# Moving two of the four attention visits in the second layer: from steps 13.5 and 21.5 to 17.5 and 24

## The chip, the cores and the metric

The kernel runs on one core of one Trainium2 chip. The metric is the device time of one execution in microseconds. Three runs of the kernel before gave a median of 938.7 us (937.01 to 938.94). The engines are named as in the profile: PE multiplies matrices (PEld loads its weights), ACT, DVE and POOL work element by element, SP issues all DMAs of the stretch that matters here.

## The reference

What is computed is causal attention with a window of 128 keys and a distance bias, for 8 sequences of 576 tokens and 8 heads of 64, and behind it a two-layer network with a mish-like gate, for all 4608 tokens (512 to 2048 to 512 wide). Cut to what matters:

```python
scores = scale * q @ k.T                       # per head, scale = 1/sqrt(64)
scores = where((rel >= 0) & (rel < 128), scores + bias, -1e9)
attn   = softmax(scores)
x      = (attn @ v)  -> [4608, 512]
h      = x @ w_in                              # 512 -> 2048
g      = h * tanh(softplus(h))
out    = g @ w_out                             # 2048 -> 512
```

## The kernel before

**Tiling.** The network takes 512 tokens at a time: one chunk `c` per sequence, 0 to 7, and a ninth chunk of the 64 tokens that are left over from each sequence. Every fp32 operand is split into a high and a low part, and three products of the parts are added up, so each layer of a chunk is 192 matmuls of 128x512. The first layer (`first`, tile `h`) makes 8 pairs of feature blocks `j`. `mish` turns `h` into `g` (ACT). `parts` splits `g` into `gg`: a high part by ACT, a low part by POOL.

**The second layer and its steps.** `second(c, half, j, t)` does six matmuls `po <- so, gg`. The 512 tokens are taken as two halves of 256, and each half as two tiles `t` of 128; a half runs through all 8 `j` with both tiles before the next half begins. So there are 32 steps of six matmuls, numbered 2m + t, where m counts 8 j's of half 0 and then 8 of half 1. Steps 0 to 15 are half 0, steps 16 to 31 half 1. The place between steps 15 and 16 is called the seam here. Each tile `t` has one bank of PSUM (`po0`, `po1`, one buffer each), so half 1 can begin to add into `po0` only when the finished sums of half 0 have been copied out of it. That copy is `store(c, half, t)`: at j = 7 it copies `po` into `ob` (for half 0 both copies are on ACT) and issues the DMA of `ob` to the output. `parts` of m stands in the program at step 2m - 4.1; `gg` has three buffers.

**The attention beside it.** While chunk c is multiplied, the attention of sequence c + 1 is done beside it, for c = 1 to 6, six layers in all. It has four pairs of heads, p = 0 to 3. For a pair: `scores` (matmuls into PSUM tile `s`), `block_bias` (DVE), `block_exp` (ACT), `divide`, `scale` (POOL), `squares_out` (a DVE transpose by 32x32 blocks, then four DMAs of `pz` to a DRAM tile `d`, two for each of two groups), `squares_in` (two DMAs of `d` back into the one buffer `pt`, in another arrangement), `values` (matmuls `o`, `w` <- `pt`, `v`), `keep` and `split_x` (copies out of PSUM). Pairs 0 and 1 are begun beside the first layer, pairs 2 and 3 beside the second. The second layer is interrupted at four places, the visits, where PE does attention matmuls: the first has the values of pair 0 and the scores of pair 2, the second the values of pair 1 and the scores of pair 3, the third the values of pair 2, the fourth the values of pair 3.

**What sets the order.** Each piece of attention has a place x in pairs, and `when(x)` maps it onto steps of the second layer, straight between the four entries of `VISITS`. The pieces and the steps are then sorted by step and written out. PE and SP keep that order (`InOrder` with `fixed`); ACT, DVE and POOL are put in order by a scheduler that goes by estimated times.

```python
steps = [(-0.001, both_scores)]
steps += [(0.01 + 0.05 * g, f) for g in range(2) for x in zip(biases[g], exps[g]) for f in x]
steps += [(0.12 + 0.09 * g, lambda g=g: weights(g)) for g in range(2)]
steps += [(0.3 + 0.15 * g, lambda g=g: squares_out(g)) for g in range(2)]
steps += [(1.005, squares_in)]
return [(p - 2 + d, f) for d, f in steps] + ends
```

These are the lines for pairs 2 and 3. `ends` are `values` at p, `keep` at p + 0.008 and `split_x` at p + 0.009. Apart from the visits, `load_v` of pair 3 stands at the fixed step 17.5. Its buffer (tag `x3`) was used by `ob` of half 0, so the load waits on SP until both output DMAs of half 0 have landed.

Of the kernel before, what the change touches and what calls it, by code (L numbers as in the profile page):

```python
# [80 lines left out]
def attention_mish_mlp(  # L81
# [225 lines left out]
    def load_pair(b, p):  # L307
        t = at.tile([P, 2 * S], F32, tag="qk", name=f"qk{b}_{p}")
        load(t, qk_[b, p][:, : 2 * S])
        qkv[(b, p)] = parts_of(t)  # L310

    def load_v(b, p):

        if b > 1:
            t = xp.tile([P, 7, P], F32, tag=f"x{p}", name=f"v{b}_{p}", bufs=1)
            load(t, v[b, p, :, :7])
            qkv[("v", b, p)] = t
            return
        if (b, p) == (0, NP - 1):
            t = begin[:, :1024].rearrange("p (a k n) -> p a k n", a=2, k=4)  # L320
        else:
            t = xp.tile([P, 2, 4, P], F32, tag=f"x{p}", name=f"v{b}_{p}", bufs=1)
        load(t.rearrange("p a k n -> p (a k) n"), v[b, p])
        qkv[("v", b, p)] = ((t[:, 0], t[:, 1]), t[:64, 1, 3])
# [654 lines left out]

    def attention(b):  # L980

        VISITS = (5.5, 13.5, 21.5, 29.9)

        def when(x):
            k = min(max(int(x // 1), 0), 2)
            return VISITS[k] + (VISITS[k + 1] - VISITS[k]) * (x - k)

        def next_pair(p):
            nxt = (b, p + 2) if p + 2 < NP else (b + 1, p + 2 - NP)
            if nxt[0] < B:  # L990
                load_pair(*nxt)

        ahead, steps = {}, []
        for p in range(NP):
            if p > 1:
                steps += pair_steps(b, p) + [(p - 1.993, lambda p=p: next_pair(p))]
                continue
            before, beside, behind, squares_in, ends = pair_steps(b, p)

            ahead[4 + 2 * p] = (before + [lambda p=p: next_pair(p)], beside, behind)  # L1000
            if p:
                steps.append((0.005, squares_in))
            else:
                ahead[5] = ([], [], [squares_in])
            steps += ends
        steps = [(when(x), f) for x, f in steps]

        steps += [(d, lambda p=p: load_v(b, p)) for p, d in enumerate((-0.5, -0.4, 6.5, 17.5))]
        return ahead, sorted(steps, key=lambda s: s[0])
# [175 lines left out]

    for c in range(1, B + 1):
        ahead, steps_beside = attention(c + 1) if c + 1 < B else ({}, [])
        for j in range(NJ):
            before, beside, behind = ahead.get(j, ([], [], []))
# [119 lines left out]
```

## Time and profile before

| | |
|---|---|
| median of three runs | 938.7 us |
| the profiled execution, its own time | 938.49 us |
| its span in the trace | 936.8 us |
| PE busy | 921.8 us, 98% of the span |
| ACT, POOL, DVE busy | 436.1, 337.9, 287.1 us |
| granted PE clock | full in all 40 slices |

About 1.7 us of the profiled time lie outside the span. To read it: PE is the engine that is never free for long, and matmuls of one kind follow each other in a pipe, so the trace shows each with some 390 ns while they start about 227 ns apart. What a place costs is read from the starts of matmuls, not from their shown lengths. Where PE sat idle, the row names in square brackets how long and what ended it.

### The profile page before, as it was taken

To read this page: it belongs to the slowest core of one execution; us is meant where nothing else is said; L and a number is where in the kernel's file an instruction comes from. 1 tells how busy PE (TensorE), PEld (TensorE's weight loads), DVE (VectorE), ACT (ScalarE), POOL (GpSimd) and SP (SyncE) were. 2 spreads that over 40 slices of the span, in tenths; PEclk is the share of its full clock that TensorE was granted. 3 is DMA by queue.
4 is the path that set the end of the run, shared out by engine and by line. 5 is a ranking of instruction groups with operands and counts; after the bars stand their busy time and mean duration, and the time that the engine had idled before them with its cause. 6 is when DMAs were issued, how large, how long until landed. Compare 5 with 4: busy or idle time off the path is not lost.

```text
span 936.8 us, 17458 instructions
## 1 busy us (share of the span) xinstructions
PE 921.8 (98%) x6842; PEld 755.6 (81%) x6842; DVE 287.1 (31%) x1095; ACT 436.1 (47%) x1075; POOL 337.9 (36%) x300
## 2 busy tenths in 40 slices
PE   8999999999999999999999999999999999999997
PEld 7788788887888788887888788878888788888886
DVE  5998760433023511332043302251042300100000
ACT  6999653744255623653265425461364422322221
POOL 4587741245123521254123512262124410331042
PEclk9999999999999999999999999999999999999999
DMA  9973210457124740546044721564055510000001
GB/s 345 392 281 116 96 54 25 127 148 216 46 65 140 205 128 15 176 137 184 25 126 120 226 65 43 162 170 140 23 157 144 160 47 1 23 23 23 0 23 24
DMA packets 79379, 108.23 MB, mean 116 GB/s; under 512 B 9280, under 2 KB 59456, under 8 KB 79296
## 3 DMA queue, kind: packets, MB, share of 16 engines
q1 hardware_dynamic: 79296, 107.11, 37.4%
q8 instruction: 54, 0.88, 0.4%
q14 instruction: 29, 0.24, 0.1%
HBM read 75.37 MB, written 31.72 MB: 114 GB/s over the span
## 4 chain that ended last, share of the span: by engine, by line
PE 89%; ACT 5%; DMA 3%; DVE 1%; issue 1%; SPq 0%; POOL 0%; ACTq 0%; DVEq 0%
PE h L69 41%; PE po L69 39%; ACT pz L69 3%; PE s L69 2%; PE o L69 2%; DMA wi<-in_moe_w_in_dram 1%; PE po0s L69 1%; PE w L69 1%; PE os L69 1%; DMA nl<-in_rell_dram 1%; DMA first<-in_qkb_dram 1%; ACT to L69 0%; ACT so L69 0%; ACT ob L69 0%; DVE to L69 0%
## 5 line engine op out<-in xcount | busy, mean ns | idle before, releaser
L69 PE MATMUL po<-so,gg 128*128 128x512 f32 x1728 | 405.5, 392 | 6.3 <-ACT ob L69 6.3
L69 PE MATMUL h<-x,si 128*128 128x512 f32 x1728 | 398.1, 390 | 0.0
L69 PEld LDWEIGHTS po<-so,gg 128*128 128x128 f32 x1728 | 321.2, 188 | 77.3 <-ACT ob L69 8.9
L69 PEld LDWEIGHTS h<-x,si 128*128 128x128 f32 x1728 | 323.0, 188 | 70.3 <-issue 3.3
L69 POOL TENSOR_TENSOR gg<-g,gg 128x512 fp32r<-128x512 f32 x144 | 185.1, 1288 | 404.5 <-ACT gg L69 404.5
L69 ACT ACTIVATE gg<-g 128x512 fp32r<-128x512 f32 x144 | 90.6, 630 | 183.9 <-PE po L69 181.8
L69 ACT ACTIVATE g<-h 128x1024 f32<-128x1024 f32 x72 | 74.0, 1028 | 193.5 <-PE h L69 193.4
L69 POOL TENSOR_TENSOR pz<-pz,sm 128x768 f32<-128x768 f32 (+3 forms) x72 | 99.0, 1384 | 128.2 <-DVE sm L69 118.5
L69 ACT ACTIVATE pz<-pz,mx 128x192 f32<-128x192 f32 (+1 forms) x280 | 120.2, 430 | 10.5 <-DVE mx L69 10.1
L69 DVE CUSTOM_DVE_ANT_0 pz<-s,nb 128x192 f32<-128x192 f32 (+1 forms) x160 | 46.7, 327 | 101.7 <-PE s L69 99.9
L69 DVE STREAM_TRANSPOSE pz<-pz 128x768 f32<-128x768 f32 (+1 forms) x48 | 51.2, 1067 | 18.0 <-POOL pz L69 18.0
L69 DVE CUSTOM_DVE_ANT_0 pz<-os,nb 128x192 f32<-128x192 f32 x24 | 8.5, 355 | 150.3 <-PE ws L69 150.3
L69 ACT ACT_TABLE_LOAD x39 | 50.0, 1283 | 5.7 <-DVE mx L69 5.3
L69 ACT ACTIVATION_READ_ACCUMULATOR pz<-pz,mx 128x1 f32 x280 | 52.3, 187 | 0.0
L69 DVE COPY ob<-po 128x512 f32<-128x512 f32 x10 | 6.9, 692 | 137.3 <-PE po L69 137.3
L69 PE MATMUL w<-pt,v 64*64 64x64 f32 (+1 forms) x864 | 41.1, 239 | 0.0
L69 DVE COPY xo<-w 128x64 f32<-128x64 f32 x24 | 5.4, 225 | 115.1 <-PE w L69 114.8
L69 PE MATMUL o<-pt,v 64*64 64x64 f32 (+1 forms) x768 | 40.4, 248 | 0.0
L69 PEld LDWEIGHTS o<-pt,v 64*64 64x64 f32 x768 | 36.8, 133 | 4.3 <-issue 4.2
L69 PEld LDWEIGHTS w<-pt,v 64*64 64x64 f32 x864 | 37.7, 133 | 0.0
L69 ACT ACTIVATE x<-o 128x256 fp32r<-128x256 f32 (+1 forms) x32 | 12.9, 403 | 43.5 <-PE w L69 42.9
L69 ACT ACTIVATE ob<-po 128x512 f32<-128x512 f32 x26 | 14.9, 599 | 34.1 <-PE po L69 34.1
(183 smaller groups left out, 581.1 us busy)
## 6 DMA issues: line engine op xcount, KB each, us to landing
qk<-in_qk_dram SPq DMA_DIRECT2D x28, 576.0 KB, 5.6
d<-pz SPq DMA_DIRECT2D x48, 240.0 KB, 3.4
pt<-d SPq DMA_DIRECT2D x24, 480.0 KB, 5.9
v<-in_v_dram SPq DMA_DIRECT2D x24, 448.0 KB, 4.4
d<-pz SPq DMA_DIRECT2D x48, 192.0 KB, 2.9
pt<-d SPq DMA_DIRECT2D x24, 384.0 KB, 4.3
wi<-in_moe_w_in_dram SPq DMA_DIRECT2D x16, 512.0 KB, 10.7
wo<-in_moe_w_out_dram SPq DMA_DIRECT2D x16, 512.0 KB, 10.2
```

The costliest lines, as they stand in the source:

```text
L69: ins = method(*args, **kwargs)
```

## The change

One line: the second visit moves from between steps 13 and 14 to between steps 17 and 18, and the third from between steps 21 and 22 to behind step 24. The first (5.5) and the fourth (29.9) stay.

```diff
     def attention(b):
 
-        VISITS = (5.5, 13.5, 21.5, 29.9)
+        VISITS = (5.5, 17.5, 24.0, 29.9)
 
         def when(x):
             k = min(max(int(x // 1), 0), 2)
             return VISITS[k] + (VISITS[k + 1] - VISITS[k]) * (x - k)
```

Everything that `when` places between the visits moves with them. Counted in steps of the second layer, the stretches between visits were 8, 8 and 8, and become 12, 7 and 5.

On ACT, at the end of half 0, the second visit of the layer beside sequence 2 stood thus before. `pz2_3` are the exponentials of pair 3, `gg1_1_1` the high part for half 1, j = 1, and `ob1_0` the output copies of half 0:

```order
L69 ACTIVATE gg1_1_0_2404<-g1_0_1775 128x512
L69 ACTIVATE gg1_1_1_2502<-g1_0_1775 128x512
L69 ACTIVATE pz2_3_0_2430,sm2_3_0_2429<-pz2_3_0_2430,mx2_3_0_2428 128x6x32 x4
L69 ACTIVATE pz2_3_1_2444,sm2_3_1_2443<-pz2_3_1_2444,mx2_3_1_2442 128x6x32
L69 ACTIVATE sm2_3_0_2429<-sm2_3_0_2429 128x4
L69 ACTIVATE pz2_3_1_2444,sm2_3_1_2443<-pz2_3_1_2444,mx2_3_1_2442 128x6x32 x2
L69 ACTIVATE pz2_3_1_2444,sm2_3_1_2443<-pz2_3_1_2444,mx2_3_1_2442 128x4x32 x2
L69 ACTIVATE sm2_3_1_2443<-sm2_3_1_2443 128x5
L69 ACTIVATE x2_1_2489<-o2_1_2445 128x256
L69 ACTIVATE x2_1_2489<-w2_1_2446 128x2x128
L69 ACTIVATE ob1_0_2524<-po1_0_0_2202 128x512
L69 ACTIVATE ob1_0_2524<-po1_0_1_2209 128x512
```

The same stretch of ACT after the change:

```order
L69 ACTIVATE gg1_1_0_2404<-g1_0_1775 128x512
L69 ACTIVATE gg1_1_1_2419<-g1_0_1775 128x512
L69 ACTIVATE ob1_0_2428<-po1_0_0_2202 128x512
L69 ACTIVATE ob1_0_2428<-po1_0_1_2209 128x512
L69 ACTIVATE gg1_1_2_2439<-g1_1_1893 128x512
L69 ACTIVATE gg1_1_3_2554<-g1_1_1893 128x512
L69 ACTIVATE pz2_3_0_2467,sm2_3_0_2466<-pz2_3_0_2467,mx2_3_0_2465 128x6x32 x4
L69 ACTIVATE pz2_3_1_2481,sm2_3_1_2480<-pz2_3_1_2481,mx2_3_1_2479 128x6x32
```

The two output copies now stand ahead of the exponentials and of the copies of `x2_1`, not behind them; two casts of `gg` come between.

On SP, where a DMA that waits holds up all that stand behind it, the same layer had this order before. `d02_3` and `d12_3` are the two groups of pair 3 in DRAM, `pt2_3` their load back, `v2_3` the values of pair 3, `qk3_1` the queries and keys of a pair of the next sequence:

```order
L69 DMA d02_2_2370<-pz2_2_0_2257 128x3x128 x2
L69 DMA d12_2_2386<-pz2_2_1_2271 128x3x160 x2
L69 DMA pt2_2_2481<-d02_2_2370 64x4x384
L69 DMA pt2_2_2481<-d12_2_2386 64x4x480
L69 DMA qk3_1_2484<-in_qk_dram 128x1152
L69 DMA xs_95<-xo2_1_2486 128x64
L69 DMA out_0_dram<-ob1_0_2524 128x512 x2
L69 DMA d02_3_2546<-pz2_3_0_2430 128x3x128 x2
L69 DMA d12_3_2564<-pz2_3_1_2444 128x3x160 x2
L69 DMA v2_3_2567<-in_v_dram 128x896
L69 DMA pt2_3_2635<-d02_3_2546 64x4x384
L69 DMA pt2_3_2635<-d12_3_2564 64x4x480
```

And after:

```order
L69 DMA d02_2_2382<-pz2_2_0_2257 128x3x128 x2
L69 DMA d12_2_2395<-pz2_2_1_2271 128x3x160 x2
L69 DMA out_0_dram<-ob1_0_2428 128x512 x2
L69 DMA v2_3_2518<-in_v_dram 128x896
L69 DMA pt2_2_2520<-d02_2_2382 64x4x384
L69 DMA pt2_2_2520<-d12_2_2395 64x4x480
L69 DMA qk3_1_2523<-in_qk_dram 128x1152
L69 DMA xs_95<-xo2_1_2525 128x64
L69 DMA d02_3_2577<-pz2_3_0_2467 128x3x128 x2
L69 DMA d12_3_2590<-pz2_3_1_2481 128x3x160 x2
L69 DMA pt2_3_2659<-d02_3_2577 64x4x384
L69 DMA pt2_3_2659<-d12_3_2590 64x4x480
```

The output DMAs and the load of `v2_3` move from between the transfers of pair 3 to ahead of the load of `pt2_2`.

## Rows read from the trace of the kernel before

**Rows 1.** The page: the span, and one group of instructions.
```profile
span 936.8 us, 17458 instructions
...
L69 PE MATMUL po<-so,gg 128*128 128x512 f32 x1728 | 405.5, 392 | 6.3 <-ACT ob L69 6.3
```
**Rows 2.** Who waited for whom, whole span: us in total, times, longest us.
```profile
PE po L69 <- ACT ob L69: 6.3, 6, 1.2
```
**Rows 3.** Timeline of PE beside sequence 3: start us, us, what, [idle before].
```profile
305.07 11.18 PE L69 MATMUL po<-so,gg 128*128 128x512 f32 x48
316.18 1.57 PE L69 MATMUL s<-qk 64*64 64x192 f32 x33
...
319.21 3.02 PE L69 MATMUL po<-so,gg 128*128 128x512 f32 x12
323.25 8.46 PE L69 MATMUL po<-so,gg 128*128 128x512 f32 x36 [1.03 <-ACT ob L69]
331.64 0.32 PE L69 MATMUL o<-pt,v 64*64 64x128 f32 x1
...
333.16 11.20 PE L69 MATMUL po<-so,gg 128*128 128x512 f32 x48
```
**Rows 4.** The chain of work that ended last: a second layer without attention.
```profile
801.50 43.52 PE po L69 x192
```
**Rows 5.** Timeline of ACT, same layer as rows 3.
```profile
316.34 0.63 ACT L69 ACTIVATE gg<-g 128x512 fp32r<-128x512 f32 x1 [2.09 <-PE po L69]
317.53 0.46 ACT L69 ACTIVATE pz<-pz,mx 128x192 f32<-128x192 f32 x1 [0.56 <-DVE mx L69]
...
322.61 1.08 ACT L69 ACTIVATE ob<-po 128x512 f32<-128x512 f32 x2
```
**Rows 6.** Timeline of POOL, same layer.
```profile
324.31 1.29 POOL L69 TENSOR_TENSOR gg<-g,gg 128x512 fp32r<-128x512 f32 x1
```
**Rows 7.** Timeline of SP's DMA issues: start us, us to issue, what.
```profile
312.87 0.53 SPq L69 DMA_DIRECT2D d<-pz  x1
...
319.35 1.71 SPq L69 DMA_DIRECT2D pt<-d  x2
...
326.87 0.55 SPq L69 DMA_DIRECT2D d<-pz  x1
...
333.30 0.58 SPq L69 DMA_DIRECT2D pt<-d  x1
334.32 1.32 SPq L69 DMA_DIRECT2D pt<-d  x1
```
**Rows 8.** DMAs issued 326.85 to 329: packets and rate; KB, us to landing.
```profile
DMA packets 898, 0.80 MB, mean 370 GB/s; under 512 B 128, under 2 KB 662, under 8 KB 898
...
d<-pz SPq DMA_DIRECT2D x1, 240.0 KB, 5.4
```
**Rows 9.** Larger load of `pt`, stretches 332 to 345 and 231 to 240.
```profile
pt<-d SPq DMA_DIRECT2D x1, 480.0 KB, 5.9
...
pt<-d SPq DMA_DIRECT2D x1, 480.0 KB, 5.5
```
**Rows 10.** The same load of `pt` at 626.76, a second visit.
```profile
626.76 1.64 SPq L69 DMA_DIRECT2D pt<-d  x1
...
pt<-d SPq DMA_DIRECT2D x1, 480.0 KB, 7.6
```
**Rows 11.** Beside sequence 6: scores of pair 3 (PE), last write of `d`.
```profile
622.89 1.57 PE L69 MATMUL s<-qk 64*64 64x192 f32 x33
...
634.39 0.36 SPq L69 DMA_DIRECT2D d<-pz  x1
```
**Rows 12.** Output DMAs, issued 323 to 324.09, and 348.1 to 350.
```profile
out_dram<-ob SPq DMA_DIRECT2D x2, 256.0 KB, 5.8
...
out_dram<-ob SPq DMA_DIRECT2D x2, 256.0 KB, 2.2
```
**Rows 13.** Write of `d` of pair 2, issued at 312.87.
```profile
d<-pz SPq DMA_DIRECT2D x1, 240.0 KB, 4.7
```

## The prediction

> **What bounds the kernel now.** The first thing to read is the page: is one engine full, and what ends its idle time? PE does nearly all of the span, and its costliest group of matmuls, the second layer's, has 6.3 us of idle time in front of it, all of it ended by an ACT copy into `ob` [rows 1]. The view of who waited for whom says how often: six times, 1.2 us at the longest [rows 2]. Nine chunks have a seam between their halves and six of them have the visits, so it is the visits that make the seam wait. The timeline of PE then shows the place: behind the second visit come twelve matmuls (steps 14 and 15), and the next one, the first of half 1, stands idle for 1.03 us [rows 3]. The timeline of ACT shows why: the cast of `gg` at 316.34 is followed by the exponentials of pair 3 from 317.53, and the two copies of `po` into `ob` come only at 322.61, behind all of them [rows 5]. Step 14 had ended at 319.21 + 1.36 = 320.57 by the step's length below, 2.0 us before. The rest of PE's time is matmuls, which the change neither adds nor removes.
>
> **What the seam costs.** A second layer without attention takes 43.52 us for 192 matmuls [rows 4], which is 0.2267 us for a matmul and 1.36 us for a step. Twelve matmuls from 319.21 would end at 321.93; the thirteenth started at 323.25 [rows 3]. So the seam costs 1.32 us, 0.29 more than the idle time shown, because the last matmul's shown length covers part of the hole. For six layers that is 6.3 + 6 x 0.29 = 8.0 us.
>
> **The part at the seam.** In the new order ACT has the two copies ahead of the exponentials. Two copies take 1.08 us [rows 5], so 0.54 each. In front of them stands a cast of 0.63 us that may begin when step 13 ends; step 14 lasts 1.36, so ACT is free when step 14 ends. The copy of `po0` is done 0.54 later, and step 15 covers it with 1.36 us. The copy of `po1` ends 0.54 us behind the seam and is wanted 1.36 behind it, under step 16. Both are covered with 0.8 us to spare; without that cover the price is again the 1.32. I take the whole 8.0 us as gained. More than that is excluded, because nothing else of PE's work changes.
>
> **What becomes late next.** Let the second visit begin at 0. It lasts 319.21 - 316.18 = 3.03 us. Between two visits, eight steps took 316.18 - 305.07 = 11.11 us [rows 3], 0.23 more than 8 x 1.36; I add that 0.23 to each stretch. Seven steps give 7 x 1.36 + 0.23 = 9.75, so the third visit begins at 12.78. It lasts 333.16 - 331.64 = 1.52 and ends at 14.30. Five steps give 7.03, so the fourth begins at 21.33. Each of these steps must find its data.
>
> *`gg` for step 24.* Its POOL half stands behind pair 3's scaling, as another did before, which ended at 324.31 + 1.29 = 325.60, that is 9.4 after the visit's start [rows 6]. Step 24 begins at 3.03 + 0.23 + 6 x 1.36 = 11.4. Covered by 2.0 us.
>
> *`pt` of pair 2, for the third visit.* `pt` has one buffer, so the load begins when the values of pair 1 are done: the first issue came 0.14 behind the visit [rows 3, 7], the second at most 1.02 behind the first (333.30 to 334.32 [rows 7]). Such a load took up to 7.6 us [rows 10]. That gives 3.03 + 0.14 + 1.02 + 7.6 = 11.8 against 12.78, so it costs nothing, with 1.0 us of cover.
>
> *`pt` of pair 3, for the fourth visit.* This is the tight one. The values of pair 2 end at 14.30; with 0.14, 1.02 and a landing of 5.5 to 5.9 [rows 9] the load is there at 20.96 to 21.36, and it is wanted at 21.33. It also has to wait until `d` of pair 3 is written. Before, its last write landed at 326.87 + 5.4 - 316.18 = 16.1 [rows 3, 7, 8], and beside sequence 6, with the same 5.4, at 634.39 + 5.4 - 622.89 = 16.9 [rows 8, 11]. But two output DMAs stood ahead of these writes and took 5.8 us to land where an empty queue gave 2.2 [rows 12]: the writes stood in a queue that was full. At the 370 GB/s of that stretch [rows 8] the 512 KB, or 0.52 MB, of output are 1.4 us. They now leave earlier, so the writes land at about 14.7, and 15.5 in the worst layer. The second load is issued at 14.30 + 0.14 + 1.02 = 15.46 anyway. So the wait is between nothing and 0.1 us a layer for most. Its lower end is zero. Its upper end is that moving the output wins nothing: 16.1 + 5.9 = 22.0 is 0.7 us late, 16.9 + 5.9 = 22.8 is 1.5 late, and five layers of the one and one of the other make 5.0 us. I take 0.4 us in all, near the lower end, because the rows of the third visit (5.5 and 5.9) were measured with the same neighbours as they will have.
>
> The Trainium skill, in "DMA: Bandwidth & Descriptors", section "Anatomy of one DMA — SWDGE (gpsimd) path", gives a DMA about 2.0 us fixed plus its bytes at 436 GB/s, most of the fixed part being the receipt of the write. By that estimate the 480 KB of `pt` would land after 3.1 us, the fourth visit would never wait, and the sum would be 930.5. The rows of this queue show 5.5 to 5.9, so the trace does not agree and is used.
>
> **The sum.** Against the profiled execution's own 938.49 us: 938.49 - 8.0 + 0.4 = 930.9 us. The median is 0.2 us from that execution, so I leave it there.
>
> **The rivals.** *The fourth visit waits.* If the writes of `d` do not land earlier, the 5.0 us above apply: 938.5 - 8.0 + 5.0 = 935.5. For it speaks that this stretch shrinks from eight steps to five and the whole path of pair 3, from its scores to its values, by 6.8 us; against it, the shorter queue.
>
> *The queue of SP (slower).* The load of `v` for pair 3 waits on SP until both output DMAs have landed, and in the new order the loads of `pt` of pair 2 stand behind it. The second output DMA is issued 2 steps less one copy before the second visit, at -2.72 + 0.54 = -2.2. If it took 5.8 us again [rows 12], it would land at 3.6; with some 0.5 us to issue the load of `v`, as for a write of `d` [rows 7], `pt` would go at 4.1 in place of 3.2, and 448 KB of `v` ahead of it cost another 1.2 us at 370 GB/s. That is 2.1 us late: then `d` lands at 16.8 and the fourth visit waits 16.8 + 5.9 - 21.3 = 1.4 us, in a bad layer more, with up to 1.1 at the third visit too. With 2.0 us a layer the time is 938.5 - 8.0 + 12.0 = 942.5. It turns the sign from 1.34 us of wait a layer on. Against it: the last write of pair 2 landed at 312.87 + 4.7 = 317.6 [rows 7, 13], 12.5 behind the end of the first visit; the first output now comes nine steps and a copy behind it, 12.8. So the queue is empty, the 2.2 us apply, and `v` can be issued at about 0.
>
> *The seam waits all the same.* If something other than the exponentials holds the copies back, the time stays 938.5. Against it: of nine seams only the six with a visit just ahead wait [rows 2].
>
> **How the numbers follow.** The forecast, 929.0 to 932.5, gets 0.74; the late fourth visit, 932.5 to 935.5, 0.11; the seam that still waits 0.06; the queue 0.09. About 0.2%, or 1.9 us, is what a measurement of this kernel can tell from no change. So faster 0.84, the same 0.07, slower 0.09. The low end, 929.0, is the whole gain, 930.5, less the 1.5 us by which the fastest run shown lies under the profiled one. The high end is the first rival's 935.5.
>
> **What would show it.** The idle time of PE in front of `po` that an ACT copy ended should fall from 6.3 us to nearly nothing, and the timeline of ACT should show `ob` ahead of `pz`. Any new loss should stand in front of the first `o` or `w` matmul of the fourth visit, ended by the DMA into `pt`; if it stands in front of the third visit, the queue of SP is the cause. Idle time at the seam, or of more than 0.3 us a layer at the fourth visit, would make the prediction wrong.

## The result

The kernel with the change took 930.64 us, against 938.67 us for the kernel before (medians of four executions each). The ratio, taken from the means, is 0.9917 with a 95% interval of 0.9898 to 0.9937. The predicted time was 930.9 us. Run once more beside nineteen other runs of the kernel before (median 937.72), it took 930.41 us, ratio 0.9921 (0.9906 to 0.9935). One of the first four executions of the changed kernel, the one that was profiled, ran from end to end at a granted PE clock of 0.555 and took 1537 us, and it is left out of the ratio; the other three took 930.35 to 930.75. All rows below are from a profiled execution of the same kernel with a mean granted clock of 0.999.

The page of that execution, its span and the group that answers to [rows 1]:

```profile
span 928.1 us, 17469 instructions
...
L69 PE MATMUL po<-so,gg 128*128 128x512 f32 x1728 | 403.7, 392 | 0.0
```

The idle time in front of the second layer's matmuls went from 6.3 us to nothing. The timeline of PE, beside sequence 3 as in [rows 3] (start us, us, engine, what):

```profile
303.21 16.62 PE L69 MATMUL po<-so,gg 128*128 128x512 f32 x72
319.76 1.57 PE L69 MATMUL s<-qk 64*64 64x192 f32 x33
...
322.79 9.82 PE L69 MATMUL po<-so,gg 128*128 128x512 f32 x42
332.54 0.32 PE L69 MATMUL o<-pt,v 64*64 64x128 f32 x1
...
334.05 7.12 PE L69 MATMUL po<-so,gg 128*128 128x512 f32 x30
341.10 0.32 PE L69 MATMUL o<-pt,v 64*64 64x128 f32 x1
```

The seam lies 60 matmuls into the run of 72, and no row breaks it there: PE goes from half 0 into half 1 without a hole. No row of the visits has an idle time either. In the kernel before, the fourth visit of this layer began here:

```profile
344.28 0.32 PE L69 MATMUL o<-pt,v 64*64 64x128 f32 x1
```

From the end of the first visit to the start of the fourth, with the same steps and visits between, PE took 344.28 - 305.07 = 39.21 us before [rows 3] and takes 341.10 - 303.21 = 37.89 us now, 1.32 us less. The timeline of ACT, which answers to [rows 5], shows the reason:

```profile
314.49 0.63 ACT L69 ACTIVATE gg<-g 128x512 fp32r<-128x512 f32 x1 [2.09 <-PE po L69]
315.79 0.60 ACT L69 ACTIVATE ob<-po 128x512 f32<-128x512 f32 x1 [0.67 <-PE po L69]
317.15 0.60 ACT L69 ACTIVATE ob<-po 128x512 f32<-128x512 f32 x1 [0.76 <-PE po L69]
317.64 0.62 ACT L69 ACTIVATE gg<-g 128x512 fp32r<-128x512 f32 x1
319.93 0.63 ACT L69 ACTIVATE gg<-g 128x512 fp32r<-128x512 f32 x1 [1.66 <-PE po L69]
321.11 0.45 ACT L69 ACTIVATE pz<-pz,mx 128x192 f32<-128x192 f32 x1 [0.55 <-DVE mx L69]
```

Each copy into `ob` now waits for PE, 0.67 and 0.76 us, where PE had waited for it. The exponentials (`pz`) come 3.4 us behind the second copy. The issues of SP in the same layer, which answer to [rows 7], and their landings by stretch (KB, us to landing), which answer to [rows 8, 9, 12]:

```profile
316.41 1.71 SPq L69 DMA_DIRECT2D out_dram<-ob  x2
...
319.84 0.34 SPq L69 DMA_DIRECT2D v<-in_v_dram  x1
...
322.93 0.58 SPq L69 DMA_DIRECT2D pt<-d  x1
...
329.98 0.47 SPq L69 DMA_DIRECT2D d<-pz  x1
...
334.90 0.81 SPq L69 DMA_DIRECT2D pt<-d  x1
```

```profile
out_dram<-ob SPq DMA_DIRECT2D x2, 256.0 KB, 2.0
...
v<-in_v_dram SPq DMA_DIRECT2D x1, 448.0 KB, 3.1
...
d<-pz SPq DMA_DIRECT2D x1, 240.0 KB, 4.2
...
pt<-d SPq DMA_DIRECT2D x1, 480.0 KB, 5.8
```

Read with the visits: the output lands in 2.0 us and `v` of pair 3 is issued at 319.84, 0.08 behind the start of the second visit, so it holds nothing up. The last write of `d` lands at 329.98 + 4.2 = 334.2, just ahead of the load that needs it (334.90). That load lands at 334.90 + 5.8 = 340.7, 0.4 us before the fourth visit at 341.10.

### The profile page after: what moved, and what is told of

It reads as the page before. It is cut to its first block, busy times and chain, and to the rows that moved or that the text cites. A ratio compares the mean times of both kernels' runs of the same rounds, so it can differ in the third digit from the quotient of the medians.

```text
span 1535.3 us, 17469 instructions
## 1 busy us (share of the span) xinstructions
PE 1528.4 (100%) x6842; PEld 905.3 (59%) x6842; DVE 289.1 (19%) x1095; ACT 439.9 (29%) x1075; POOL 336.8 (22%) x300
## 4 chain that ended last, share of the span: by engine, by line
PE 99%; DMA 0%; SPq 0%; ACT 0%; issue 0%
PE h L69 43%; PE po L69 43%; PE s L69 4%; PE o L69 4%; PE w L69 1%; PE po0s L69 1%; PE os L69 1%; DMA first<-in_qkb_dram 0%; PE po1s L69 0%; PE pt_0l L69 0%; PE pt_2l L69 0%; PE pt_3l L69 0%; PE pt_1l L69 0%; PE warm L69 0%; PE ws L69 0%; SPq L69 0%
## 5 line engine op out<-in xcount | busy, mean ns | idle before, releaser
L69 PE MATMUL po<-so,gg 128*128 128x512 f32 x1728 | 672.6, 575 | 0.0
L69 PE MATMUL h<-x,si 128*128 128x512 f32 x1728 | 669.6, 576 | 0.0
L69 PEld LDWEIGHTS h<-x,si 128*128 128x128 f32 x1728 | 375.6, 218 | 286.3 <-issue 172.9
L69 PEld LDWEIGHTS po<-so,gg 128*128 128x128 f32 x1728 | 375.2, 219 | 274.1 <-issue 161.3
L69 PE MATMUL w<-pt,v 64*64 64x64 f32 (+1 forms) x864 | 65.8, 306 | 0.0
L69 PE MATMUL o<-pt,v 64*64 64x128 f32 (+1 forms) x768 | 65.7, 325 | 0.0
L69 PEld LDWEIGHTS o<-pt,v 64*64 64x64 f32 x768 | 56.4, 159 | 13.6 <-issue 8.4
L69 PEld LDWEIGHTS w<-pt,v 64*64 64x64 f32 x864 | 56.7, 161 | 0.0
L69 ACT ACT_TABLE_LOAD x39 | 50.0, 1283 | 11.3 <-DVE mx L69 10.8
L69 PE MATMUL s<-qk 64*64 64x192 f32 (+1 forms) x560 | 43.5, 462 | 0.0
L69 ACT ACTIVATE ob<-po 128x512 f32<-128x512 f32 x26 | 15.5, 598 | 83.5 <-PE po L69 83.5
## 6 DMA issues: line engine op xcount, KB each, us to landing
wi<-in_moe_w_in_dram SPq DMA_DIRECT2D x16, 512.0 KB, 10.7
```

Source lines behind the costliest of these rows:

```text
L69: ins = method(*args, **kwargs)
```

## The experiments

An edit is against the changed kernel unless the text says otherwise, and "over the changed kernel" means over its 930.41 us. The runs were taken on two chips, on which the kernel before took 937.72 and 938.12 us.

**The changed kernel again.** No edit.

> The changed kernel once more, unaltered, for a trace at the full PE clock. Theory (the gain is the wait at the seam, 1.32 us a layer, and the fourth visit hardly waits): 930.6 us; no idle time of PE in front of po that an ACT copy ended; idle time in front of the fourth visit under 0.3 us a layer. Rival (the seam still waits a little and another wait has shrunk): idle time in front of po after step 15 stays at some tenths of a us a layer.

930.41 us, and no idle time of PE anywhere between the first and the last of the visits. The rival falls, since nothing is left in front of `po`; so does the small wait that I had allowed for at the fourth visit.

**Only the second visit moved.**

```diff
-        VISITS = (5.5, 17.5, 24.0, 29.9)
+        VISITS = (5.5, 17.5, 21.5, 29.9)
```

> Only the second visit moves (17.5), the third stays at 21.5. Between them are 4 steps, 4 x 1.36 + 0.23 = 5.67 us. The larger load of pt of pair 2 landed 0.14 + 0.7 to 1.0 + 5.5 to 7.6 = 6.3 to 8.8 us behind the visit. Theory (the DMA round trip needs its steps): the third visit waits 0.7 to 3.1 us a layer, about 1.3, so 930.6 + 8 = 938.6 us (935 to 945). Rival (the loads of pt have slack, and the third visit was moved for nothing): 930.6 us.

941.21 us, ratio to the kernel before 1.0028 (1.0015 to 1.004): slower than before. The ten executions lie between 938.41 and 942.84 us. Who PE waited for, from 195 to 760 us (us, times, longest), in the profiled execution of 942.53 us:

```profile
PE w L69 <- DMA pt<-d: 7.2, 6, 2.8
PE o L69 <- DMA pt<-d: 0.4, 1, 0.4
```

Right behind the longest of these waits, which ended at 231.71, PE stood thus (stretch, its length, PE busy, granted clock, share of the DMA engines, GB/s):

```profile
231.80:235.10 3.30, 3.30 (x68) 0.50 0.40 126
```

The wait at `ob` is gone, and in its place stands a wait for the load of `pt` in every layer. By itself the move of the second visit gains at the seam and loses more than that at the third visit: 10.8 us over the changed kernel in the median. Not all of it is waiting. Behind that longest wait the granted clock fell to 0.5, the level of 1.2 GHz; by the rows of the run "One step further ahead" below, I estimate that at 1.6 us. The three shortest executions, 938.41 to 938.70 us at a mean granted clock of 0.998 to 0.999, are the 938.6 that was expected; the other seven have 0.996 to 0.998. The rival falls: the third visit had to go with it.

**Only the third visit moved.**

```diff
-        VISITS = (5.5, 17.5, 24.0, 29.9)
+        VISITS = (5.5, 13.5, 24.0, 29.9)
```

> Only the third visit moves (24), the second stays at 13.5. Theory (the whole gain is at the seam, and the third visit's move only makes room for the load of pt of pair 2): the seam waits as before, the fourth visit has five steps and hardly waits, 938 us as before, within 1 us. Rival (moving the third visit gains something of its own): under 936 us.

937.62 us, ratio 0.9998 (0.9988 to 1.0007): no change. From 140 to 760 us PE waited for this and nothing else:

```profile
PE po L69 <- ACT ob L69: 6.1, 6, 1.0
```

The wait at the seam is what it was [rows 2], and five steps ahead of the fourth visit cost nothing. So the third visit's move gains nothing of its own.

**The scores of pair 3 moved alone.** The kernel before with its visits, and pair 3's scores, exponentials and what follows in a fifth place behind the seam:

```diff
+            if p == 3:
+                for x, f in pair_steps(b, p) + [(p - 1.993, lambda p=p: next_pair(p))]:
+                    if x < 1.9:
+                        apart.append((16.5 + 6.5 * (x - 1), f))
+                    else:
+                        steps.append((x, f))
+                continue
...
         steps = [(when(x), f) for x, f in steps]
+        steps += apart
```

> The kernel before with its visits at 13.5 and 21.5, but the scores of pair 3 and all that follows from them moved away from the second visit, to a visit of their own at step 16.5, behind the seam. Theory (the exponentials ahead of the output copies on ACT are the whole cause of the wait at the seam): the gain of 8.0 us appears, less 0.23 us for a fifth interruption in each of six layers, 938.7 - 8.0 + 1.4 = 932 us. Rival (the gain comes from the values of pair 1, or from the output DMAs leaving the queue earlier): the seam waits as before and the time is 938.7 + 1.4 = 940 us.

932.38 us, ratio 0.9942 (0.9928 to 0.9957), where 932 was expected. The values of pair 1 still stand at 13.5, and the output DMAs still follow the load of `pt`. The timeline of ACT at the seam:

```profile
315.34 0.63 ACT L69 ACTIVATE gg<-g 128x512 fp32r<-128x512 f32 x1 [2.09 <-PE po L69]
318.38 0.60 ACT L69 ACTIVATE ob<-po 128x512 f32<-128x512 f32 x1 [0.88 <-PE po L69]
319.76 0.60 ACT L69 ACTIVATE ob<-po 128x512 f32<-128x512 f32 x1 [0.78 <-PE po L69]
...
322.36 0.45 ACT L69 ACTIVATE pz<-pz,mx 128x192 f32<-128x192 f32 x1 [1.48 <-DVE mx L69]
```

PE waited for nothing in the six layers. Its timeline, at the end of the first visit and at the start of the fourth:

```profile
304.06 11.18 PE L69 MATMUL po<-so,gg 128*128 128x512 f32 x48
...
342.37 0.32 PE L69 MATMUL o<-pt,v 64*64 64x128 f32 x1
```

Taking the scores of pair 3, and with them the exponentials, out of the copies' way is enough for the whole gain, less the cost of the additional interruption. That cost is 342.37 - 304.06 = 38.31 us against 37.89 in the changed kernel, so 0.42 us a layer where 0.23 was allowed for. The rival, that the gain came from the values or from the DMA queue, falls.

**The second visit at the seam itself.**

```diff
-        VISITS = (5.5, 17.5, 24.0, 29.9)
+        VISITS = (5.5, 15.5, 23.0, 29.9)
```

> The second visit at 15.5, exactly at the seam, the third at 23 (eight steps apart, six before the fourth). On ACT both output copies still stand ahead of the exponentials. Theory (what matters is the order of the copies and the exponentials on ACT, not on which side of the seam the visit is): 930.4 us, no wait. Rival (the visit has to stand behind the first steps of half 1, since ACT and PSUM need them): a wait of 0.5 us or more a layer in front of po, 933.5 us or more.

930.51 us, ratio 0.9915 (0.99 to 0.993), the same as the change. The timeline of ACT:

```profile
315.27 0.60 ACT L69 ACTIVATE ob<-po 128x512 f32<-128x512 f32 x1 [0.67 <-PE po L69]
316.63 0.60 ACT L69 ACTIVATE ob<-po 128x512 f32<-128x512 f32 x1 [0.76 <-PE po L69]
...
317.88 0.46 ACT L69 ACTIVATE pz<-pz,mx 128x192 f32<-128x192 f32 x1
```

The visit begins as the last step of half 0 ends, and that is late enough. Two steps are not needed behind the seam; what is needed is that both copies are ahead of the exponentials.

**One step further ahead.**

```diff
-        VISITS = (5.5, 17.5, 24.0, 29.9)
+        VISITS = (5.5, 14.5, 22.0, 29.9)
```

> The second visit at 14.5, one step further ahead, the third at 22. On ACT the copy of po0 stands ahead of the exponentials, the copy of po1 behind them and behind two copies of x. Theory: po1 is copied at about 6.5 to 7.0 us behind the visit's start and wanted by step 17 at 3.03 + 0.23 + 2 x 1.36 = 6.0, so step 17 waits some 1.1 us a layer, 930.4 + 6.6 = 937 us. Rival (only po0 at the seam can wait): 930.4 us.

942.82 us, ratio 1.005 (1.0033 to 1.0068), 12.4 us over the changed kernel where 6.6 were expected. Who PE waited for from 140 to 760 us, and the timeline of ACT beside sequence 3:

```profile
PE po L69 <- ACT ob L69: 9.2, 6, 2.6
```

```profile
317.90 0.60 ACT L69 ACTIVATE ob<-po 128x512 f32<-128x512 f32 x1 [0.67 <-PE po L69]
319.14 0.46 ACT L69 ACTIVATE pz<-pz,mx 128x192 f32<-128x192 f32 x1 [0.64 <-DVE mx L69]
...
324.22 0.59 ACT L69 ACTIVATE ob<-po 128x512 f32<-128x512 f32 x1
```

The copy of `po0` is in time, that of `po1` stands behind the exponentials and comes 6.3 us later. So `po1` can wait as `po0` did, and the rival falls. The size was off: four layers waited 1.02 us, two waited 2.57. In one of these two, beside sequence 4, the timeline of ACT and that of DVE show what came on top:

```profile
425.58 0.37 ACT L69 ACTIVATE x<-o 128x256 fp32r<-128x256 f32 x1
427.74 0.38 ACT L69 ACTIVATE x<-w 128x256 fp32r<-128x256 f32 x1 [1.79 <-DVE xo L69]
428.02 0.59 ACT L69 ACTIVATE ob<-po 128x512 f32<-128x512 f32 x1
```

```profile
426.47 0.98 DVE L69 STREAM_TRANSPOSE pz<-pz 128x768 f32<-128x768 f32 x1 [0.57 <-POOL pz L69]
427.48 0.23 DVE L69 COPY xo<-w 128x64 f32<-128x64 f32 x1
```

There the scheduler put DVE's copy `xo` behind a transpose, ACT's copy of `w` waited 1.79 us for it, and the copy of `po1` stood behind that. These waits, 9.2 us as shown and 0.29 more a layer for the pipe, make 10.9 of the 12.4 us. In the profiled execution the clock explains the rest. The other wait of 2.57 us stands beside sequence 6; behind it, PE and its granted clock were:

```profile
634.69 10.06 PE L69 MATMUL po<-so,gg 128*128 128x512 f32 x36 [2.57 <-ACT ob L69]
```

```profile
635.10:638.50 3.40, 3.40 (x10) 0.50 1.00 334
```

PE came out of the wait at 634.69, and from 635.1 to 638.5 the granted clock was 0.5, the level of 1.2 GHz. The 36 matmuls took 10.06 us, where 36 took 8.46 in [rows 3]: 1.6 us more, which brings the sum to 12.5. Behind the equal wait beside sequence 4 the clock did not fall.

**The output DMAs put back behind the load of `pt`.** The changed kernel, with the copies into `ob` early but their DMAs, and the load of `v` of pair 3, in their old places on SP:

```diff
-        steps += [(d, lambda p=p: load_v(b, p)) for p, d in enumerate((-0.5, -0.4, 6.5, 17.5))]
+        steps += [(d, lambda p=p: load_v(b, p)) for p, d in enumerate((-0.5, -0.4, 6.5, 20.5))]
+        steps.append((17.6, lambda: [unsent.pop(0)() for _ in range(len(unsent))]))
...
+        def send():
+            for k, rows in rows_of(c, 2 * half + t):
+                sp.dma_start(out=rows, in_=ob[k])
+
+        if 0 < c < B - 1 and half == 0:
+            unsent.append(send)
+        else:
+            send()
```

> The changed kernel with the two output DMAs of half 0 and the load of v of pair 3 put back where they stood on SP before, between the transfers of pair 3; the copies into ob stay early. Theory (the output ahead of the writes of d makes them land 1.4 us later, and the fourth visit has no room for that): d lands at about 16 us behind the second visit's start, the fourth visit waits 0.3 to 0.6 us in the layers that also load qk, 932 to 934 us. Rival (the order on SP's queue does not matter to the fourth visit): 930.4 us.

932.6 us, ratio 0.9944 (0.9927 to 0.9962): 2.2 us over the changed kernel. Who PE waited for from 140 to 760 us:

```profile
PE w L69 <- DMA pt<-d: 0.4, 1, 0.4
```

Beside sequence 3, the scores of pair 3 on PE, and on SP the last write of `d`, the load of `v` and the second load of `pt`:

```profile
320.71 1.57 PE L69 MATMUL s<-qk 64*64 64x192 f32 x33
```

```profile
330.74 0.50 SPq L69 DMA_DIRECT2D d<-pz  x1
333.34 0.34 SPq L69 DMA_DIRECT2D v<-in_v_dram  x1
...
335.95 0.57 SPq L69 DMA_DIRECT2D pt<-d  x1
```

```profile
d<-pz SPq DMA_DIRECT2D x1, 240.0 KB, 5.1
...
pt<-d SPq DMA_DIRECT2D x1, 480.0 KB, 6.3
```

The write lands at 330.74 + 5.1 - 320.71 = 15.1 us behind the start of the visit, where the changed kernel has 334.2 - 319.76 = 14.4. The load behind it lands at 342.2, 21.5 behind that start, and the fourth visit stands at 21.3. Only one of the waits at the fourth visit is long enough to be shown; by the starts of matmuls, `po` before the visit to `po` behind it, four of the six layers are longer than in the changed kernel, by 0.1, 0.3, 0.4 and 0.8 us, which is 1.5 of the 2.2 us. So the queue's order does matter to the fourth visit, and the rival falls.

The way is for the most part another than the expected one. The later `d` puts off the issue of this load by 0.1 us only (335.95 - 320.71 = 15.24 against 334.90 - 319.76 = 15.14); the larger part is its landing, 6.3 us against 5.8, with the load of `v` issued just ahead of it. The delay of `d` itself is 0.7 us, half of the 1.4 expected; it was issued 0.2 earlier behind the visit's start and took 0.9 longer to land. Why it is not 1.4 is open.

**The third visit one step later.**

```diff
-        VISITS = (5.5, 17.5, 24.0, 29.9)
+        VISITS = (5.5, 17.5, 25.0, 29.9)
```

> As the changed kernel, with the third visit at step 25 in place of 24: four steps, 5.67 us, before the fourth visit in place of five, 7.03. Theory (the load of pt of pair 3 needs 6.3 to 7.1 us behind the third visit and five steps just hold it): the fourth visit waits 0.6 to 1.4 us a layer, 4 to 8 us in all, 934.5 to 939 us. Rival (a load of 480 KB takes about 3.1 us, as the fixed part and the bytes of the Trainium skill, DMA: Bandwidth & Descriptors, section Anatomy of one DMA, give it): no wait, 930.6 us.

936.24 us, ratio 0.9983 (0.9973 to 0.9992), 5.8 us over the changed kernel. Who PE waited for from 195 to 760 us, and PE beside sequence 3:

```profile
PE w L69 <- DMA pt<-d: 4.2, 6, 0.9
```

```profile
341.69 0.43 PE L69 MATMUL o<-pt,v 64*64 64x128 f32 x2
343.04 0.29 PE L69 MATMUL w<-pt,v 64*64 64x128 f32 x1 [0.92 <-DMA pt<-d]
```

Two matmuls `o` of the fourth visit start, then `w` waits: the smaller load of `pt` is there and the larger is not. Four steps are too few and five are enough. The estimate by the Trainium skill ("DMA: Bandwidth & Descriptors", section "Anatomy of one DMA — SWDGE (gpsimd) path"), 3.1 us for this load, would have given no wait. That section's figure is for DMAs that GpSimd issues, and these are issued by SP; every one of the six layers waited, so for this queue the measurement decides.

## Why the prediction was right

*What bounds the kernel, and what the seam costs.* The price was read from the starts of matmuls, 1.32 us a layer and 8.0 in all, not from the 6.3 us of idle time shown. The medians differ by 938.67 - 930.64 = 8.03 us in the first comparison and by 937.72 - 930.41 = 7.3 in the second, with an interval of 5.9 to 9.6 for the first. The interval alone does not separate 8.0 from 6.3; the traces do, with 39.21 - 37.89 = 1.32 us in the layer beside sequence 3. The cause is shown by scores_apart, which has the gain with the values, the third visit and the output DMAs in their old places, and by third_only, which has the third visit's move and no gain. The reason given for the 0.29 us that the idle time does not show covers about half of it: the last matmul's shown length beyond its slot is 0.39 - 0.23 = 0.16 us. The rest lies behind the hole, where the second matmul starts 0.34 us after the first and not 0.23:

```profile
323.25 0.50 PE L69 MATMUL po<-so,gg 128*128 128x512 f32 x1 [1.03 <-ACT ob L69]
323.59 0.62 PE L69 MATMUL po<-so,gg 128*128 128x512 f32 x2
```

The same 0.34 stands behind each visit. The working left it out behind the hole and behind the visit too, and so 1.32 came out right.

*The part at the seam.* Expected were copies that end 0.54 behind their step, with 0.8 us to spare. The rows show 0.60 each, and ACT idle in front of both. Right; a copy alone is 0.06 longer than half of a pair, since 1.08 for two was an overlapped pair.

*What becomes late next.* The third visit was put at 12.78 behind the second and came at 332.54 - 319.76 = 12.78; the fourth at 21.33 and came at 341.10 - 319.76 = 21.34. So steps of 1.36 and 0.23 for an interruption carry over to visits that are moved whole (a visit split in two cost 0.42 more, in scores_apart). The load of `pt` of pair 3 was placed between 20.96 and 21.36 and landed at 340.7 - 319.76 = 20.9: the second issue followed the first by 0.70 and not by the 1.02 that I had taken from one layer, and `d` was written at 14.4, not 14.7. The 0.4 us allowed for the fourth visit's wait was not needed; this is the one term that failed, and it is small.

*The queue.* That the output's move lets `d` land earlier was right in direction. From 16.1 before to 14.4 it is 1.7 us; out_late gives 0.7 of it to the places of the output DMAs and of the load of `v`, half of the 1.4 in the prediction. Of the other 1.0, 0.7 is a later issue before, 326.87 - 316.18 = 10.7 behind the visit's start [rows 3, 7] against 330.74 - 320.71 = 10.0 in out_late, and 0.3 a longer landing, 5.4 us [rows 8] against 5.1. SP had waited 0.5 us for the copy into `ob` in front of these writes, and did not in out_late, so the late copies are a candidate for that issue; no run separates them. That 14.7 came so near to 14.4 is in part luck.

*The rivals.* The seam did not wait, so the third rival falls. The queue of SP did not hold the loads up: the output landed in 2.0 us, as the empty queue promised, and `v` was issued at 0.08. The late fourth visit did not happen, but third_25 and out_late show how near it is: one step less, or the old order on SP, and it waits. With the second visit at 15.5 and the third at 23 the time is the same and the fourth visit has six steps, so that placing has the same gain with more room.

## What to carry to other kernels

A copy that frees an accumulator must not stand, on an engine that works in order, behind a long list that was released just before it; moving the list a few steps is enough, and the place to look is who stands ahead of the copy, not how long the copy is. Read the price of such a wait from the start of one matmul to the start of the next, since the idle time shown was 1.03 of 1.32 us here. When interruptions are pushed together, work out for each round trip through DRAM how many steps it needs: here five held it and four cost a microsecond a layer, and moving one visit without the next turned the gain into a loss.

## What was not expected of the hardware

DMAs of like size landed after very unlike times in a queue with little in it: 2.0 us for 256 KB of output and 3.1 for 448 KB of `v`, but 5.8 for 480 KB of `pt`, which has only the smaller half of `pt` ahead of it. That smaller half, 384 KB, took 4.3 us, issued when the last write of `d` landed. While both loads ran, all packets of the queue were under 2 KB; of the 144 packets of `v`, 128 were over. No run here separates the size of its pieces from its source in DRAM.

A long wait of PE can cost more than its own length. Behind one of the two waits of 2.57 us in second_145, and behind the one of 2.84 us in second_only, the granted clock fell from 1 to 0.5 for 3.4 us, which cost 1.6 us more in second_145. Behind the other wait of 2.57 us, and behind those of 1.0 to 1.2 us in the kernel before, it stayed at 1. What decides this the runs do not show.
